# The second pass of a first stage rearranged, and TensorE's last jump made to wait, in a fused attention and gated feed-forward kernel

## The chip, the cores and the metric

The kernel runs on one core of one Trainium2 chip. The metric is the device time of one execution in microseconds (us). A core has five engines that run their own instruction streams and wait for one another through semaphores: TensorE (PE in the profile; PEld is its weight load), VectorE (DVE), ScalarE (ACT), GpSimd (POOL) and SyncE (SP). SP computes nothing here; it issues DMAs in a fixed order.

## The reference

One layer: normalise the rows of `x` (2048 rows of 640), run attention with 32 heads over given keys and values, run a gated feed-forward on the same normalised rows, and join the two.

```python
x = A_x                                   # [1, 2048, 640] bfloat16
xn = _layernorm(x, axis=-1)
# attention: H = 32 heads, Dh = 192, 2048 keys
q = (xn @ wq).reshape(B, Sq, H, Dh).transpose(0, 2, 1, 3)
scores = einsum("bhqd,bhkd->bhqk", q, k_cache) * (Dh ** -0.5)
s = (softmax(scores) @ v_cache) ... @ wo
# feed-forward: F = 1536
g = silu((silu(xn @ w1) * (xn @ w3)) @ w2)
return x + s * g
```

## The kernel before, in words

**Tiling.** The 2048 query rows are 16 row tiles of 128 (index `i`), or four blocks of 512 (`qb`). A head's 2048 keys are 16 key tiles, worked in 8 pairs (`p` from 0 to 7): tile `p` and tile `p + 8` together. One *group* is one head and one block of 512 queries, that is 8 pairs.

**One pair** is a call of `advance` (L525). It issues the scores on TensorE (`scores`, six matmuls, L467) into a PSUM tile `st2` of which there are two; the exponential on ScalarE (`weights`, L474, 1.1 us), which frees that PSUM tile; and it appends eight *pieces* (`values`, L499; two matmuls each, L507) of the product with the values to the list `parts`. Pieces are taken off the front of the list until a set number is left, so TensorE works on products of an earlier pair while ScalarE forms the exponential of this one. How many are left is the threshold in L542: 12, or 14 or 16 where other work goes in between.

**The end of a group.** The products of a group lie in two PSUM banks (`ob0`, `ob1`). When the last piece of a bank is issued, `evict` (L477) makes VectorE sum the bank's two halves into `osum` (L483, about 0.95 us); the next group's first pieces write the same bank and wait for it. The rest of it, a reciprocal (L489) and a multiplication that normalises (L490), goes to the list `late`. `drain_late`, at the start of `advance`, issues what is in `late` as soon as both banks are there.

**The start.** While the first groups run, the rows aren't all normalised yet. For a row tile `i` these steps follow each other: `ln_stats` (three instructions on VectorE, L223 and L224), `ln_root` (two on ScalarE for several tiles at once, L230 and L233), `ln_scale` (one on VectorE, L241, 128x640), `dma_turn` (a transposing DMA that SP issues, L252, into `xnT`). The first four tiles are turned on TensorE instead, between *fillers*: matmuls on constants that write a scratch bank (`keep_busy`, L210 to L217), 17 in all, issued before and between the first real matmuls. The projection of a head's queries for one block (`project_chunk`, L326; two parts of ten matmuls) needs the four turned tiles of that block. Behind it, ScalarE casts it out of PSUM, GpSimd copies rows (L359, L365), VectorE takes maxima (L353), and GpSimd sums over partitions (L424) to give a bound `nb` that the exponentials of that group read.

**The order by hand.** In this stage each instruction stands in its engine's program order as written (`pin`). The first eight groups are worked in the order

```python
order = ((0, 0), (1, 0), (0, 1), (0, 2), (0, 3), (1, 1), (1, 2), (1, 3))   # (head, qb); n is the place in it
```

and two tables say what is issued besides: `extras[(n, p)]` goes at the end of pair `p` of the `n`-th group's `advance`, `posts[(n, p)]` right after it. The *second pass* is `n = 1`: head 1, block 0. At its pair 5 the projection of head 0, block 1 begins, whose rows are tiles 4 to 7; its second part goes at pair 6 (list `seconds`). Between the two parts ScalarE holds a marker that waits for the end of the first.

**The end.** The output is formed row tile by row tile (`output_tile`, L804 for the matmuls, L809 and L811 on VectorE, L813 the store). The last tile is worked in two pieces, of 512 and 128 columns, each stored by itself from SP. Then all engines load a flag (`redo`) and jump over a part that is run only when the flag is set (L958); in this kernel's runs it isn't. A hint marks TensorE's jump as likely taken, and the engines meet at the end of the program (L1010).

Of the kernel before, what the change touches and what calls it, by code (L numbers as in the profile page):

```python
# [9 lines left out]
ALU = mybir.AluOpType  # L10
# [13 lines left out]
def _pieces(n, maxw=512):  # L24
    k = -(-n // maxw)
    w = -(-n // k)
    return [(c, min(c + w, n)) for c in range(0, n, w)]


def _kernel_impl(ctx, tc, A_x, A_k_cache, A_v_cache, A_wq, A_wo, B_w1, B_w3, B_w2, out):  # L30
    nc = tc.nc
    _, SQ, D = A_x.shape
    _, H, SK, dh = A_k_cache.shape
# [7 lines left out]
    NPAIR = NKT // 2  # L41
# [23 lines left out]
    pin = tc.keep_in_program_order  # L65
# [102 lines left out]
    with ExitStack() as actx:  # L168
# [12 lines left out]
        mv = lnx.tile([P, NQT, nc.vector.BN_AGGR_DIM], F32, name="mv")  # L181
        x_all = lnx.tile([P, NQT, D], BF16, name="x_all")
# [25 lines left out]
        one_l, one_r = (nc.const_aps.tensor(1.0, (P, w), BF16) for w in (P, 512))  # L208

        def keep_busy(n, out=None, behind=None):  # L210
            for _ in range(n):
                mm = pin(nc.tensor.matmul(fill[:, 0, :] if out is None else out, lhsT=one_l, rhs=one_r, start=True, stop=True))
                if behind:
                    tc.add_manual_dep(mm.ins, behind.ins.name,
                                      mybir.DependencyInfo(mybir.DependencyClass.Sync, mybir.DependencyReason.DATA),
                                      reason="not all at once")
                    behind = None  # L217
# [8 lines left out]
        rstd = {}  # L226
# [9 lines left out]

        scaled = {}

        def ln_scale(i):
            scaled[i] = xnp.tile([P, D], BF16, tag="xn", name="xn")  # L240
            pin(nc.vector.tensor_scalar(out=scaled[i][:], in0=x_all[:, i, :], scalar1=mv[:, i, 0:1], scalar2=rstd[i],  # L241
                                        op0=ALU.subtract, op1=ALU.mult))

        def ln_turn(i, pool, tag, cp):
# [6 lines left out]
        def dma_turn(i):  # L251
            pin(nc.sync.dma_start_transpose(out=xnT[:, i, :, :], in_=scaled.pop(i)[:]))  # L252

        def scale_and_turn(i):
            ln_scale(i)
            dma_turn(i)

        def stats_on_scalar(i):
# [266 lines left out]
        def advance(hd, qb, p, extra=None, st2=None, hold=False):  # L525
            def drain_late():
                while len(late) > 1:
                    late.pop(0)()
                    if len(late) == 1:
                        late.pop(0)()  # L530

            casts_first = p == 2 and (hd["h"] == H - 1 or (hd["h"], qb) == (1, NQB - 1)) and seconds
            if not casts_first:
                drain_late()
            first = (hd["h"], qb, p) == (0, 0, 0)
            pT2 = weights(scores(hd, qb, p) if st2 is None else st2, hd["nb"][qb], (0, 256, 512, 1024) if first else (0, 1024))
            parts.extend(values(hd, qb, p, pT2, first))
            while seconds:
                seconds.pop(0)()
            if casts_first:  # L540
                drain_late()
            while len(parts) > (16 if extra and p == 1 else 14 if extra or hold else 12):  # L542
                parts.pop(0)()
            if extra:
                extra()
# [66 lines left out]
        def complete_third():  # L612
# [19 lines left out]
            (0, 2): ((ln_root, 4), (scale_and_turn, 4), (scale_and_turn, 5), (key_maxima, 1, 0), (folded_maxima, 1)),  # L632
            (0, 4): ((join_maxima, 1), (next_bound, 1, 0)),
            (0, 5): ((ln_stats, 6), (ln_stats, 7)),
            (1, 0): ((ln_root, 6),),
            (1, 1): ((scale_and_turn, 6), (scale_and_turn, 7), (load_x, nc.sync, 12, 16)),
            (1, 2): ((ln_stats, 8), (ln_stats, 9)),
            (1, 3): ((ln_stats, 10), (ln_stats, 11)),
            (1, 4): ((ln_root, 8, 4), (scale_and_turn, 8), (scale_and_turn, 9)),
            (1, 5): ((scale_and_turn, 10), (scale_and_turn, 11)),  # L640
            (2, 2): ((ln_stats, 12), (ln_stats, 13)),
            (2, 3): ((ln_stats, 14),),
            (2, 4): ((ln_stats, 15),),
# [8 lines left out]
        def first_passes(n0, n1):  # L652
            for n in range(n0, n1):
                h, qb = order[n]
                for p in range(NPAIR):
                    todo = extras.get((n, p))
                    advance(heads[h], qb, p, (lambda: [f(*a) for f, *a in todo]) if todo else None,
                            early.pop(0) if early else None, (p == 0 and (n, 1) in extras) if n else p > 1)
                    for f, *a in posts.get((n, p), ()):
                        f(*a)  # L660
                    if n >= 6 and p > 2 and key_slots:
                        key_maxima(2, *key_slots.pop(0))
                    if p > 4 and gated:
                        gated.pop(0)()
                    if (n, p) == (7, 6):
                        assert not key_slots
                        finish_head(2)
                if n == 7:
                    while gated:
                        gated.pop(0)()  # L670
# [124 lines left out]
    def output_tile(pools, i, oT, xt):  # L795
        dsb, _, dps = pools
        split = i == NQT - 1
        to = nc.sync if split else nc.scalar
        ps_s = [dps.tile([P, 1024], F32, tag="st2", name="ps_s") for _ in range(2 if split else 1)]
        cuts = ((0, 512), (512, D)) if split else DP  # L800
        pieces = [(ps_s[-pi if split else 0][:, pi * 512:pi * 512 + c1 - c0], c0, c1) for pi, (c0, c1) in enumerate(cuts)]
        order = [(k, q) for q in pieces for k in range(OC)] if split else [(k, q) for k in range(OC) for q in pieces]
        for k, (ps, c0, c1) in order:
            pin(nc.tensor.matmul(ps, lhsT=oT[:, k, :], rhs=wo_sb[:, k, c0:c1], start=(k == 0), stop=(k == OC - 1)))  # L804
        res = dsb.tile([P, D], BF16, tag="res", name="res")
        for ps, c0, c1 in pieces:
            w = c1 - c0
            tmp = dsb.tile([P, 512], F32, tag="tmp", name="tmp")
            pin(nc.vector.scalar_tensor_tensor(out=tmp[:, 0:w], in0=ps, scalar=0.25, in1=g_all[:, i, c0:c1],  # L809
                                               op0=ALU.mult, op1=ALU.mult))  # L810
            pin(nc.vector.tensor_tensor(out=res[:, c0:c1], in0=tmp[:, 0:w], in1=xt[:, c0:c1], op=ALU.add))  # L811
            if i >= NQT - 7:
                stored = to.dma_start(out=out2[i * P:(i + 1) * P, c0:c1], in_=res[:, c0:c1])  # L813
                if split and c0 == 0:
                    tc.add_manual_dep(stored.ins, acc["out"].ins.name,
                                      mybir.DependencyInfo(mybir.DependencyClass.Sync, mybir.DependencyReason.DATA),
                                      reason="the tiles ahead are stored ahead")
                acc["out"] = stored
        if i < NQT - 7:
            to.dma_start(out=out2[i * P:(i + 1) * P, :], in_=res[:])  # L820
# [16 lines left out]
    with ExitStack() as dctx:  # L837
        dsb = dctx.enter_context(tc.tile_pool(name="dsb", bufs=3))
        otp = dctx.enter_context(tc.tile_pool(name="otp", bufs=3))
        pools = (dsb, otp, ps_st)  # L840
        with tc.issue_after(acc["store"].ins):
            tiles = [load_tile(pools, i) for i in range(3)]
        for qb in range(NQB):
            if qb + 1 < NQB:
                for fl in range(1 if qb == 0 else 0, FC - FCP):
                    ffn_hidden(qb + 1, fl, tail_ps("ps_gu"))()
            for i in range(qb * 4, qb * 4 + 4):
                ffn_out(i)
            if qb + 2 < NQB:
                load_hT(qb + 2)  # L850
            if qb == 0:
                worst = fsb.tile([P, 1], F32, tag="worst", name="worst")
                pin(nc.vector.tensor_reduce(out=worst[:], in_=rl_all[:], axis=AX.X, op=ALU.max))
                bad = fsb.tile([P, 1], BF16, tag="bad", name="bad")
                pin(nc.vector.tensor_scalar(out=bad[:], in0=worst[:], scalar1=RL_MAX, scalar2=None, op0=ALU.is_gt))
            if qb == 1:
                ps_b = ps_st.tile([P, 1024], F32, tag="st2", name="ps_b")
                pin(nc.tensor.matmul(ps_b[:, 0:1], lhsT=ones_bf[:], rhs=bad[:], start=True, stop=True))
                pin(nc.vector.tensor_copy(out=flag_i[:], in_=ps_b[:, 0:1]))
        for i in range(NQT - 1):  # L860
            output_tile(pools, i, *tiles.pop(0))
            if i + 3 < NQT:
                tiles.append(load_tile(pools, i + 3))
        with tc.block():
            tc.mark_branch_hint_location("redo", "LikelyTaken", (mybir.EngineType.PE,))
            output_tile(pools, NQT - 1, *tiles.pop(0))
    pstack.close()

    redo = nc.values_load(flag_i[0:1, 0:1], min_val=0, max_val=P)
# [145 lines left out]
```

## Time and profile before

| | us |
|---|---|
| median of three runs | 1941.05 |
| lowest and highest | 1939.77 and 1941.24 |
| the profiled execution, in all | 1939.65 |
| its span, first to last instruction | 1937.9 |
| granted TensorE clock | 0.999 |
| scores (L467), six groups by operands, each matmul | 0.376 |
| exponential (L474), 1016 of them | 1131.2 in all, 1.114 each |
| products (L507), 16384 of them | 861.4 in all, 0.243 each |
| scaling of a row tile on VectorE (L241) | 0.4 |
| GpSimd row copies, 64x512 and 64x1024 | 0.62 and 1.03 to 1.09 |

The span is the time from the first to the last instruction of the profiled execution; the rest of its 1939.65 us lies around it. In the tables a line gives the kernel's line, the engine, the operation, and `out<-in` by the program's names; `[0.71 <-DMA xnT<-xn]` says that the engine stood idle for 0.71 us before it, until the DMA that writes `xnT` had landed. Matmuls are pipelined, so one of 0.376 us starts every 0.1 to 0.2 us.

### The profile page before, as it was taken

The page shows a single profiled execution, that of the slowest core. Times are in us where ns is not written, and L with a number is a line of the kernel's source. Part 1 is how long each engine was busy: PE and PEld are TensorE (multiplying, and loading weights), DVE is VectorE, ACT ScalarE, POOL GpSimd, SP SyncE. Part 2 cuts the span into 40 slices and gives each one's busy share as a digit, 9 for nine tenths or more (in the row PEclk, how much of TensorE's full clock was granted, in tenths as well). Part 3 has the DMA queues.
Part 4 walks back from the last instruction along what each step waited for, and adds up shares of the span by engine and source line. Part 5 has one row for each costly group of instructions (what it writes and reads, how often), then busy time and mean ns, then how long its engine had stood idle before and what let it go on. Part 6 is the DMA issues. An engine that isn't in the chain of part 4 may idle for free.

```text
span 1937.9 us, 60322 instructions
## 1 busy us (share of the span) xinstructions
PE 1928.0 (99%) x27227; PEld 1359.5 (70%) x27228; DVE 1022.3 (53%) x1861; ACT 1278.7 (66%) x1296; POOL 414.3 (21%) x634
## 2 busy tenths in 40 slices
PE   8999999999999999999999999999999999999998
PEld 5779866666666777766666666677776666677776
DVE  8475556565656565556555565555565544521111
ACT  6777777777777777777777777777777777210000
POOL 2422222222222222222222222222222110000000
PEclk9999999999999999999999999999999999999999
DMA  8532323232222222333423232323232102927782
GB/s 180 105 76 53 79 47 85 47 74 45 67 45 71 52 67 60 63 82 77 109 57 75 55 77 55 76 47 85 47 85 44 40 5 75 287 65 135 151 155 54
DMA packets 361575, 152.83 MB, mean 79 GB/s; under 512 B 312448, under 2 KB 355136, under 8 KB 361312
## 3 DMA queue, kind: packets, MB, share of 16 engines
q1 hardware_dynamic: 346736, 120.11, 28.7%
q0 software_dynamic: 7872, 23.60, 4.8%
q10 hardware_dynamic: 6704, 5.21, 1.0%
q8 instruction: 214, 3.51, 0.7%
q14 instruction: 49, 0.40, 0.1%
HBM read 56.23 MB, written 31.98 MB: 46 GB/s over the span
## 4 chain that ended last, share of the span: by engine, by line
PE 98%; SPq 1%; DVE 1%; DMA 0%; ACT 0%; POOL 0%; issue 0%; POOLq 0%
PE obank L507 35%; PE st L467 34%; PE ps L326 14%; PE ps_s L804 11%; PE ps_f L828 3%; PE ps_gu L310 1%; SPq L124 0%; PE ps_gu L326 0%; DMA KB<-in_A_k_cache_dram 0%; DVE st L223 0%; DVE osum L483 0%; ACT pT L474 0%; SPq L185 0%; DVE mv L224 0%; DVE st L396 0%
## 5 line engine op out<-in xcount | busy, mean ns | idle before, releaser
L474 ACT ACTIVATE pT<-st,nb 128x1024 bf16<-128x1024 f32 x1016 | 1131.2, 1114 | 346.0 <-PE st L467 339.8
L507 PEld LDWEIGHTS <-pT 64*128 64x128 bf16 x16384 | 731.1, 94 | 225.0 <-issue 0.9
L507 PE MATMUL obank<-vt,pT 64*128 64x193 bf16 x16384 | 861.4, 243 | 0.3
L483 DVE TENSOR_REDUCE osum<-obank 128x386 f32<-128x772 f32 x256 | 234.4, 957 | 584.7 <-PE obank L507 584.6
L467 PE MATMUL st<-qA,KA 64*128 64x512 bf16 x2048 | 398.2, 376 | 1.1 <-ACT pT L474 1.0
L467 PE MATMUL st<-qF,KB 64*128 64x512 bf16 x1024 | 385.0, 376 | 0.0
L467 PE MATMUL st<-qS,KC 64*128 64x512 bf16 x1024 | 384.9, 376 | 0.1
L467 PE MATMUL st<-qS,KB 64*128 64x512 bf16 x1024 | 384.9, 376 | 0.0
L467 PE MATMUL st<-qD,KC 64*128 64x512 bf16 x960 | 361.0, 376 | 0.0
L326 PE MATMUL ps<-xnT,w 64*128 64x512 bf16 x2520 | 315.8, 376 | 0.7 <-DMA xnT<-xn 0.7
L359 POOL COPY qS<-qA 64x512 bf16<-64x512 bf16 x256 | 159.6, 623 | 636.2 <-ACT qA L369 627.7
L467 PEld LDWEIGHTS <-KC 64*128 64x128 bf16 x1984 | 186.2, 94 | 104.9
L326 PEld LDWEIGHTS <-w 64*128 64x128 bf16 x2520 | 132.4, 94 | 110.3 <-issue 1.1
L804 PE MATMUL ps_s<-wo_sb,oT 128*128 128x320 bf16 (+2 forms) x1535 | 208.8, 299 | 0.1
L467 PEld LDWEIGHTS <-KB 64*128 64x128 bf16 x2112 | 193.4, 94 | 13.6 <-issue 0.6
L804 PEld LDWEIGHTS <-oT 128*128 128x128 bf16 x1536 | 148.4, 98 | 60.4
L490 DVE TENSOR_TENSOR ostage<-osum,rl_all 128x384 bf16<-128x384 f32 x256 | 158.0, 617 | 8.8
L467 PEld LDWEIGHTS <-KA 64*128 64x128 bf16 x2048 | 116.7, 93 | 17.4 <-issue 2.7
L105 POOL DMA_DIRECT2D w<-in_A_wq_dram x60 | 53.1, 885 | 286.2 <-PE ps L326 286.0
L370 DVE CAST qF<-ps 128x512 bf16<-128x512 f32 x120 | 82.9, 691 | 51.6 <-ACT qA L369 51.6
L809 DVE SCALAR_TENSOR_TENSOR tmp<-ps_s,g_all 128x320 f32<-128x320 f32 (+2 forms) x32 | 15.6, 488 | 176.0 <-PE ps_s L804 176.0
L353 DVE TENSOR_REDUCE st<-qA 128x1 f32<-128x512 bf16 x128 | 86.5, 676 | 8.7 <-ACT qA L369 8.7
(95 smaller groups left out, 1035.4 us busy)
## 6 DMA issues: line engine op xcount, KB each, us to landing
o_scr<-ostage SPq DMA_DIRECT2D x64, 384.0 KB, 2.7
vt<-in_A_v_cache_dram SPq DMA_DIRECT2D x31, 768.0 KB, 6.3
wo_sb<-in_A_wo_dram POOLq DMA_DIRECT2D x1, 7680.0 KB, 32.2
w<-in_A_wq_dram POOLq DMA_DIRECT2D x30, 160.0 KB, 3.4
hT_scr<-hblk SPq DMA_DIRECT2D x16, 256.0 KB, 2.9
xt<-in_A_x_dram POOLq DMA_DIRECT2D x16, 160.0 KB, 8.8
w<-in_B_w_dram POOLq DMA_DIRECT2D x30, 80.0 KB, 2.6
w<-in_A_wq_dram POOLq DMA_DIRECT2D x30, 80.0 KB, 2.7
```

Of the source, the lines that this page charges most:

```text
L105: return lambda eng: keep(eng.dma_start(out=w[:, :, c0:c1], in_=src[:, s0:s0 + c1 - c0].rearrange("(c p) d -> p c d", p=P)))
L326: mm = pin(nc.tensor.matmul(out[:, t * 512:(t + 1) * 512], lhsT=ws[t][ROWS[r], c, :], rhs=rows_of(qb, c, ROWS[r]), start=(ph == 0 and c == 0),
L353: pin(nc.vector.tensor_reduce(out=hd["st"][r0:P, 2 + s, qb:qb + 1], in_=src[r0:P, qb * 512:(qb + 1) * 512], axis=AX.X, op=ALU.max, apply_a ...
L359: return [lambda t=t: keep(nc.gpsimd.tensor_copy(out=hd["qS"][ROWS[t], qs], in_=hd["qA"][ROWS[1 - t], qs])) for t in range(2)]
L370: pin(cast(out=hd["qF"][:, qs], in_=ps[:, 512:1024]))
L467: pin(nc.tensor.matmul(st2[:, t * 512:(t + 1) * 512], lhsT=keys, rhs=q[ROWS[t], qs], start=(s == 0), stop=(s == 2)))
L474: pin(nc.scalar.activation(out=pT2[:, c0:c1], in_=st2[:, c0:c1], func=ACT.Exp, scale=SCALE, bias=nb[:]))
L483: pin(nc.vector.tensor_reduce(out=osum[:], in_=ob[:].rearrange("p t (j c) -> p j c t", j=2)[:, :, 0:DH + 1, :], axis=AX.X, op=ALU.add))
L490: pin(nc.vector.tensor_tensor(out=ostage[:, b * 2:b * 2 + 2, hg * DH:(hg + 1) * DH], in0=osum[:, :, 0:DH], in1=rl.unsqueeze(2).to_broadcas ...
L507: pin(nc.tensor.matmul(acc["o"][b][:, r, j * 256:j * 256 + DH + 1], lhsT=pT2[ROWS[r], t * 512 + i * P:t * 512 + (i + 1) * P], rhs=vt[ROWS[ ...
L804: pin(nc.tensor.matmul(ps, lhsT=oT[:, k, :], rhs=wo_sb[:, k, c0:c1], start=(k == 0), stop=(k == OC - 1)))
L828: pin(nc.tensor.matmul(ps[:, pi * 512:pi * 512 + c1 - c0], lhsT=hT[:, fc, qsl], rhs=w2_sb[:, fc, c0:c1], start=(fc == 0), stop=(fc == FC - ...
```

## The change

Five edits.

- **Fillers in halves.** `keep_busy` issues each filler as two matmuls of 256 columns instead of one of 512.
- **Scaling.** `ln_scale` and `scale_and_turn` take an engine. Row tile 6 is scaled on GpSimd, right after the root of tiles 6 and 7 at the end of pair 0 of the second pass, instead of on VectorE at pair 1. The root of tiles 8 to 11 and the scaling and turning of tiles 8 and 9 go from the end of pair 4 to the end of pair 5, where tiles 10 and 11 already were.
- **Normalising put back.** In the second pass the first group's normalising (`late`) isn't issued at pair 2, but at pair 6, the seventh.
- **Pieces held.** In the second and third group 16 pieces instead of 12 are left in the list at pair 1. (The new condition gives the same as before in all other groups.)
- **The last jump.** Behind the last output tile TensorE gets an empty instruction that waits for VectorE's last sum; the flag's load and the jump stand behind it.

```diff
         def keep_busy(n, out=None, behind=None):
-            for _ in range(n):
-                mm = pin(nc.tensor.matmul(fill[:, 0, :] if out is None else out, lhsT=one_l, rhs=one_r, start=True, stop=True))
+            to = fill[:, 0, :] if out is None else out
+            for c0, c1 in _pieces(512, 256) * n:
+                mm = pin(nc.tensor.matmul(to[:, c0:c1], lhsT=one_l, rhs=one_r[:, c0:c1], start=True, stop=True))
...
-        def ln_scale(i):
+        def ln_scale(i, eng=nc.vector):
             scaled[i] = xnp.tile([P, D], BF16, tag="xn", name="xn")
-            pin(nc.vector.tensor_scalar(out=scaled[i][:], in0=x_all[:, i, :], scalar1=mv[:, i, 0:1], scalar2=rstd[i],
+            pin(eng.tensor_scalar(out=scaled[i][:], in0=x_all[:, i, :], scalar1=mv[:, i, 0:1], scalar2=rstd[i],
                                         op0=ALU.subtract, op1=ALU.mult))
...
-        def scale_and_turn(i):
-            ln_scale(i)
+        def scale_and_turn(i, eng=nc.vector):
+            ln_scale(i, eng)
             dma_turn(i)
...
             casts_first = p == 2 and (hd["h"] == H - 1 or (hd["h"], qb) == (1, NQB - 1)) and seconds
-            if not casts_first:
+            put_back = (hd["h"], qb) == (1, 0) and p < NPAIR - 2
+            if not casts_first and not put_back:
                 drain_late()
...
-            while len(parts) > (16 if extra and p == 1 else 14 if extra or hold else 12):
+            while len(parts) > (16 if p == 1 and (extra or hold) else 14 if extra or hold else 12):
...
-            (1, 0): ((ln_root, 6),),
-            (1, 1): ((scale_and_turn, 6), (scale_and_turn, 7), (load_x, nc.sync, 12, 16)),
+            (1, 0): ((ln_root, 6), (scale_and_turn, 6, nc.gpsimd)),
+            (1, 1): ((scale_and_turn, 7), (load_x, nc.sync, 12, 16)),
             (1, 2): ((ln_stats, 8), (ln_stats, 9)),
             (1, 3): ((ln_stats, 10), (ln_stats, 11)),
-            (1, 4): ((ln_root, 8, 4), (scale_and_turn, 8), (scale_and_turn, 9)),
-            (1, 5): ((scale_and_turn, 10), (scale_and_turn, 11)),
+            (1, 5): ((ln_root, 8, 4), (scale_and_turn, 8), (scale_and_turn, 9), (scale_and_turn, 10), (scale_and_turn, 11)),
...
-                            early.pop(0) if early else None, (p == 0 and (n, 1) in extras) if n else p > 1)
+                            early.pop(0) if early else None, (p == ((n, 1) not in extras)) if n else p > 1)
...
-            pin(nc.vector.tensor_tensor(out=res[:, c0:c1], in0=tmp[:, 0:w], in1=xt[:, c0:c1], op=ALU.add))
+            acc["sum"] = pin(nc.vector.tensor_tensor(out=res[:, c0:c1], in0=tmp[:, 0:w], in1=xt[:, c0:c1], op=ALU.add))
...
             output_tile(pools, NQT - 1, *tiles.pop(0))
+            wait = pin(nc.tensor.nop())
+            tc.add_manual_dep(wait.ins, acc["sum"].ins.name,
+                              mybir.DependencyInfo(mybir.DependencyClass.Sync, mybir.DependencyReason.DATA),
+                              reason="what follows the jump is fetched behind the last rows")
```

## The prediction

> **What bounds the kernel now.** I read the first page of the profile first, then the busy times by stage, then the order of time around the one stage that isn't full, then the end.
>
> ```profile
> span 1937.9 us, 60322 instructions
> PE 1928.0 (99%) x27227; PEld 1359.5 (70%) x27228; DVE 1022.3 (53%) x1861; ACT 1278.7 (66%) x1296; POOL 414.3 (21%) x634
> PE 98%; SPq 1%; DVE 1%; DMA 0%; ACT 0%; POOL 0%; issue 0%; POOLq 0%
> ```
>
> TensorE is busy 1928.0 of 1937.9 us and nearly alone on the chain that ends last, so an edit can win only out of the 9.9 us in which it stands still, whatever it does elsewhere. The busy times by stage (stretch and its length, then busy us of PE, its weight loads, DVE, ACT, POOL, with instruction counts) say where those are.
>
> ```profile
> 24.00:44.00 20.00, 18.01 (x276) 12.68 (x272) 15.37 (x40) 14.03 (x18) 2.55 (x5) 1.00 0.85 147
> 44.00:70.00 26.00, 26.00 (x391) 18.42 (x387) 14.31 (x38) 20.90 (x24) 7.45 (x13) 1.00 0.65 110
> 70.00:1600.00 1530.00, 1530.00 (x23616) 1087.96 (x23613) 885.17 (x1571) 1170.55 (x1149) 385.25 (x581) 1.00 0.28 63
> 1724.00:1938.00 214.00, 208.90 (x1538) 148.37 (x1536) 31.11 (x66) 0.88 (x2) 7.02 (x13) 0.99 0.62 119
> ```
>
> From 44 us to 1724 us nothing is missing. What the change can reach is the 2.0 us lost between 24 and 44 us (the second pass, head 1) and the 5.1 us at the end, 4.9 of them after the last matmul (1932.95). The timeline of the second pass:
>
> ```profile
> 30.61 1.23 SPq L252 DMA_TRANSPOSE xnT<-xn  x1
> 33.43 1.25 PE L326 MATMUL ps<-xnT,w 64*128 64x512 bf16 x10 [0.71 <-DMA xnT<-xn]
> 33.88 0.21 DVE L224 BATCH_NORM_AGGREGATE mv<-st 128x2 f32<-128x12 f32 x1
> 34.12 0.30 ACT L230 ACTIVATE lv<-mv,eps_t 128x4 f32<-128x4 f32 x1 [2.06 <-DVE mv L224]
> 34.56 1.10 ACT L474 ACTIVATE pT<-st,nb 128x1024 bf16<-128x1024 f32 x1
> 34.69 1.51 DVE L241 TENSOR_SCALAR xn<-x_all,mv,rstd 128x640 bf16<-128x640 bf16 x4 [0.60 <-ACT rstd L233]
> 35.71 0.39 PE L467 MATMUL st<-qA,KA 64*128 64x512 bf16 x2 [1.03 <-ACT pT L474]
> ```
>
> Two stalls. The projection (33.43) waits 0.71 for the turned rows of tile 7. Then the scores at 35.71 wait 1.03 for an exponential that ScalarE began late, at 34.56, because the root of tiles 8 to 11 (34.12) stands ahead of it in ScalarE's order and waits 2.06 us for VectorE's statistics. VectorE is late for this reason:
>
> ```profile
> 26.16 1.86 DVE L483 TENSOR_REDUCE osum<-obank 128x386 f32<-128x772 f32 x2
> 27.94 0.79 DVE L241 TENSOR_SCALAR xn<-x_all,mv,rstd 128x640 bf16<-128x640 bf16 x2
> 28.65 0.16 DVE L489 RECIPROCAL rl_all<-osum 128x2 f32<-128x2 f32 x1
> 28.84 0.56 DVE L490 TENSOR_TENSOR ostage<-osum,rl_all 128x384 bf16<-128x384 f32 x1
> ```
>
> **Part by part.** *Fillers.* 17 fillers (11+2+1+1+2) become 34 of half the width, the same columns. Each of the 17 added matmuls costs nothing if its weight load hides, at most one 128x128 load (98 ns, the row of L804) if it does not: 1.1 us on the first eleven, which end ahead of a 1.14 us idle, the others beside idles of 0.38 and 0.24 us. Only the single one between two turned tiles (7.82) has no cover: up to +0.1; a shorter last piece could win as much. I take 0.
>
> *Tile 6 on GpSimd, one step earlier.* VectorE scales tiles 6 and 7 at 27.94, 0.4 us each, and SP issues their turns behind: from 28.40 (2.1 us) and 30.61 (1.23 us); by their times to landing (4.1 and 2.7 us) they land at 32.5 and 33.3. Now GpSimd scales tile 6 as soon as ScalarE's root (26.66, 0.20 us) is there, at 26.9. No such row exists on POOL; its nearest are copies, 0.62 us for 512 columns and 1.03 to 1.09 for 1024, so 0.72 for 640 by the line between them, and twice that, 1.44, if the two arithmetic steps cost two passes. POOL has idle time until 38.37, so nothing queues behind it. SP's turn of tile 6 then starts 0.75 to 0.05 us earlier. VectorE still scales tile 7, at 28.0, well before SP wants it. But the two turns before it, issued at 23.11 and 25.08, landed only at 31.3 and 31.9 (8.2 and 6.8 us): the DMA engines were behind, and turned tiles then came 0.6 us apart. By that cadence tile 7 lands at 33.1 at best, not 32.55. So the gain is 0 to 0.71 us; I take 0.2, the cadence being the nearer row.
>
> *Root of tiles 8 to 11 one pair later, normalising put back.* The exponential of pair 5 no longer stands behind the root, so it starts at 32.1, right behind its scores (31.40 plus 0.65). The scores at 35.71 could then follow the projection's first part directly, where 1.2 us lie between by the starts (33.43 plus 1.08 is 34.51): gain 1.2. The four normalising steps (0.16+0.56, twice; 1.4 us) leave VectorE's order at 28.65, so its statistics of tiles 8 to 11 end by 33.3 (x_all lands only at 29.2, and four tiles of 1.0 us follow) instead of 34.1. They come back at pair 6, and there they are on a path: the root waits behind ScalarE's marker for the first part's end (34.3), then root 0.5, scaling 1.5, normalising 1.4, and only then the query maximum, at 37.8, where its input would be ready at 36.7. GpSimd's copies run beside it, and the second maximum is wanted at 38.05 and starts at 38.45, so 0.4 us of the 1.1 reach the bound and the exponential waiting for it (41.34 before, 40.1 after). The loss is bounded by 0 (if the copies hide it) and 1.1. SP's four turns of tiles 8 to 11 keep their order; they are wanted only at 46.7 and landed at 42.5.
>
> *Pieces held.* Eight matmuls move from pair 1 to pair 2 in the second and third groups. The 0.26 us stall in the products at 26.5 (1.12 us for 16 instead of 0.85) goes, but both sums end on VectorE at 28.0 whatever TensorE does, and the held pieces then reach the second bank at 27.83: 0.2 us of waiting takes its place. In the third group the wait for the exponential at 40.1 does the same. Gain 0 to 0.4, taken as 0.1.
>
> Start in sum: 0.2 + 1.2 + 0.1 - 0.2 (what the late bound gives back by the time the next group runs full) = 1.3 us, between 0 and 2.4.
>
> *TensorE's last jump.* The views of the end (throughput in 50 ns slices from 1934 to 1936; the line of the jump; the last two stores):
>
> ```profile
> GB/s 0 0 0 0 0 0 0 0 0 31 154 220 144 57 10 328 0 0 0 0 0 0 164 0 0 0 0 0 0 0 0 0 0 0 5 5 10 5 10 5
> q8 instruction: 1, 0.02, 3.0%
> L958 PEldq COMPARE_BRANCH  x1: 1603/1603/1603, 1932.4 to 1932.4; - x1
> DMA to landing us min/median/max: 2.0/2.6/3.2
> ```
>
> The last store's rows move at 1934.45 to 1934.75, then a 16 KB instruction packet (the 328) takes one DMA engine, and the last rows come 1.0 us late, at 1935.7 to 1936.0. This store lands 3.2 us after issue, the one ahead 2.0. The jump ends at 1934.0 and the packet follows 0.77 us later. A wait for the last sum (1933.32 plus 0.29) ends at 1933.65; behind it on TensorE stand the flag's load (0.49) and the jump, so the jump ends at 1934.3 at the earliest, and its packet starts at 1935.1, behind rows that are through at 1934.75. Then the store lands 1.2 us sooner, and since every engine's end follows it, the span loses 1.2. Bounds: 0 (the packet is still served first; it must have held the engine before the slice in which it shows) and 1.25; a later TensorE matters only past 1936.9, where SP collects it. I take 1.2, because the shift of 0.3 us equals the length of the rows' burst.
>
> [...]
>
> Sum: 1937.9 - 1.3 - 1.2 = 1935.4 us of span. The profiled execution took 1939.65 in all, 1.4 below the median of 1941.05 (the three runs spread over 1.5). Taken from the median: **1938.5 us**.
>
> **Rivals.** *The end keeps its wait:* the packet still goes ahead of the rows, as it did with a jump only 0.3 us earlier: 1941.05 - 1.3 = 1939.75. For it speaks that its data were seen only after the rows' burst, though it blocked them. *The start's gain turns into a new wait:* VectorE's normalising and the exponential's bound eat the 1.3; only the end wins: 1939.85. Against it: 0.6 us of slack beside GpSimd's copies. *All stalls of the second pass vanish:* the DMA engines are less behind with SP's earlier issue, 0.7 more from the projection, 0.9 from the waits at 39.8 and 41.8: 1936.9. *GpSimd is slow at its first arithmetic:* if the scaling takes T, tile 6 is turned from 26.9+T instead of 28.40, and everything behind follows. With 2.4 us won elsewhere (1.1+1.2+0.1) it costs more than it brings from T = 3.9. At 7.5 us the kernel takes 1941.05 + 3.6 = 1944.7. Against it: POOL's first 1024-column copy took 1.03 us, no more than the later ones.
>
> [...]
>
> **How the numbers follow.** Forecast 0.45, end keeps its wait 0.22, start gives nothing 0.13, all stalls vanish 0.11, slow GpSimd 0.05, neither part does anything (1941) 0.04. A measurement of this kernel tells about 0.2% (3.9 us) from no change: faster is below 1937.2, slower above 1944.9. Faster is most of "all vanish" and the low edge of the forecast, 0.16; slower is half of the slow GpSimd and a mishap not seen, 0.06; the rest 0.78. The range goes from the fourth case to the run spread above the second and third: 1936.8 to 1941.5; the forecast's own is 1937.3 to 1939.7.
>
> **What would show it.** In the profile after: no root ahead of the sixth exponential, and scores directly behind the projection's first part; a POOL row of the scaling under 1.5 us; a wait for xnT still there, 0.4 to 0.8 us; a last store that lands in 2.0 us, not 3.2. It is wrong if TensorE waits over 1 us for xnT, if the exponential of the third group starts after 41, or if the store stays at 3.2.

## The result and the profile after

The change made the kernel slower: 1951.92 us (median of six runs, 1951.2 to 1954.1) against 1939.91 us for the kernel before (six runs, 1939.09 to 1941.24), a ratio of 1.0063 with a 95% interval of 1.005 to 1.0076. Forecast were 1938.5 us, in a range that ended at 1941.5. The profiled execution of the changed kernel is the slowest of its six (1954.1 us); that of the kernel before took 1939.65. So the two spans below lie 14.3 us apart, and the medians 12.0.

The first page and the stages of the changed kernel (a stretch and its length, then busy us of PE, its weight loads, DVE, ACT and POOL, the granted TensorE clock, the DMA share and GB/s):

```profile
span 1952.2 us, 60363 instructions
PE 1934.3 (99%) x27244; PEld 1364.8 (70%) x27245; DVE 1021.8 (52%) x1860; ACT 1277.8 (65%) x1296; POOL 416.3 (21%) x635
24.00:44.00 20.00, 13.51 (x176) 8.56 (x174) 9.90 (x29) 9.56 (x13) 3.08 (x3) 0.84 0.58 127
44.00:70.00 26.00, 20.34 (x266) 14.33 (x264) 13.41 (x35) 13.26 (x17) 4.52 (x8) 0.86 0.18 42
70.00:1600.00 1530.00, 1530.00 (x23606) 1088.99 (x23604) 884.09 (x1571) 1170.47 (x1150) 387.71 (x585) 1.00 0.29 65
```

From 70 to 1600 us TensorE is full in both kernels. The loss lies between 24 and 70 us, but for 0.7 us of a later start, and in both stages two things are new: TensorE stands still for over 5 us, and its granted clock is below 1. What TensorE waited for between 30 and 60 us (us in total, times, longest), and when GpSimd worked (start, duration):

```profile
PE ps L327 <- DMA xnT<-xn: 6.3, 1, 6.3
PE st L468 <- ACT pT L475: 5.6, 1, 5.6
```

```profile
25.23 0.38 POOL L425 PARTITION_ALL_REDUCE nb<-ns  x1 [0.77 <-DVE ns L423]
33.19 2.52 POOL L242 TENSOR_SCALAR xn<-x_all,mv,rstd 128x640 bf16<-128x640 bf16 x1 [7.58 <-PE st L468]
45.70 0.61 POOL L360 COPY qS<-qA 64x512 bf16<-64x512 bf16 x1 [9.99 <-ACT qA L370]
46.36 0.60 POOL L366 COPY qD<-qF 64x512 bf16<-64x512 bf16 x1
46.91 0.61 POOL L360 COPY qS<-qA 64x512 bf16<-64x512 bf16 x1
53.80 0.40 POOL L425 PARTITION_ALL_REDUCE nb<-ns  x1 [6.28 <-DVE st L224]
```

The scaling of tile 6 has its last input when ScalarE writes the root at 27.62, but it begins at 33.19; the sum over partitions has its input at 48.06 (the row of L423, 47.91 plus 0.15), but it begins at 53.80. The releasers that the rows name, TensorE's scores and VectorE's statistics, have nothing to do with these instructions: the inference from semaphores found the last event it knew. What does stand there are instructions that count as no work, two to configure GpSimd ahead of the scaling and two ahead of the sum:

```profile
L242 POOLq MODIFY_POOL_CONFIG  x2: 79/81/83, 25.5 to 25.5; - x2
```

```profile
L425 POOLq MODIFY_POOL_CONFIG  x2: 4/4/4, 47.7 to 47.8; - x2
```

In the kernel before and in the changed one, the line that loads a library for the sums over partitions (`load_library`, L72) shows as such a pair, at 0.8 us:

```profile
L72 POOLq MODIFY_POOL_CONFIG  x2: 11/11/11, 0.8 to 0.9; - x2
```

So I read the two pairs as GpSimd swapping the routines that it has ready, and call a pair with the idle time behind it a swap: there, to the scaling (7.6 us from the pair at 25.5), and back, to the sum (6.0 us from the pair at 47.8). The rows show the configuring instructions and the idle time behind them, not what happens in it; the experiments test when this time is paid. TensorE's two waits (6.3 and 5.6 us) are each about as long as a swap, and behind the first of them TensorE runs at half clock for 4.6 us, behind the second for 5.9 us (in a row, the clock stands after the five engines, ahead of the DMA share):

```profile
33.20:39.70 6.50, 0.22 (x6) 0.00 (x0) 1.20 (x5) 0.93 (x1) 2.51 (x1) 0.83 0.29 54
39.70:44.40 4.70, 4.65 (x24) 1.97 (x26) 1.60 (x6) 1.52 (x3) 0.00 (x0) 0.51 0.47 139
49.60:55.40 5.80, 0.21 (x4) 0.00 (x0) 5.61 (x16) 1.16 (x2) 0.40 (x1) 0.92 0.22 68
55.40:61.30 5.90, 5.89 (x54) 4.39 (x55) 0.73 (x3) 3.19 (x3) 0.00 (x0) 0.50 0.01 3
```

The sum of it: 0.7 us of a later start (first scores at 14.16 for 13.49), 5.6 us more wait for xnT (6.3 for 0.7), 5.6 for the late bound, and about half of 4.6 and of 5.9 us to the low clock, 5.3 together; that is 17.2. Off it go 1.0 for the scores' wait that is gone and 1.35 at the end (last matmul to the end of the span: 3.58 us after, 4.93 before). Left are 14.9, for 14.3 us between the spans. Marks on TensorE's way close it better: the first scores start 0.7 us later than before, the projection's first part 6.3 (39.75 for 33.43), the products behind its second part 7.3 (44.77 for 37.44), those of the next group 15.7 (65.20 for 49.48), and the last matmul ends 15.7 later as well (1948.67 for 1932.95). Less 1.35 at the end this is 14.4.

### The profile page after: what moved, and what is told of

Same layout as the page of the kernel before. It is cut to its first block, busy times and chain, and to the rows that moved or that the text cites. A ratio compares the mean times of both kernels' runs of the same rounds, so it can differ in the third digit from the quotient of the medians.

```text
span 1952.2 us, 60363 instructions
## 1 busy us (share of the span) xinstructions
PE 1934.3 (99%) x27244; PEld 1364.8 (70%) x27245; DVE 1021.8 (52%) x1860; ACT 1277.8 (65%) x1296; POOL 416.3 (21%) x635
## 4 chain that ended last, share of the span: by engine, by line
PE 98%; DVE 1%; SPq 0%; DMA 0%; POOL 0%; issue 0%; ACT 0%; POOLq 0%
PE obank L508 34%; PE st L468 34%; PE ps L327 14%; PE ps_s L805 11%; PE ps_f L829 3%; PE ps_gu L311 1%; PE ps_gu L327 0%; SPq L124 0%; DVE st L224 0%; DVE osum L484 0%; DMA w<-in_A_wq_dram 0%; DMA xnT<-xn 0%; POOL xn L242 0%; PE pa L311 0%; DVE st L354 0%
## 5 line engine op out<-in xcount | busy, mean ns | idle before, releaser
L468 PEld LDWEIGHTS <-KB 64*128 64x128 bf16 x2112 | 193.7, 94 | 14.5 <-issue 1.6
L491 DVE TENSOR_TENSOR ostage<-osum,rl_all 128x384 bf16<-128x384 f32 x256 | 157.2, 614 | 8.8
```

The lines of the kernel that those rows point to most:

```text
L468: pin(nc.tensor.matmul(st2[:, t * 512:(t + 1) * 512], lhsT=keys, rhs=q[ROWS[t], qs], start=(s == 0), stop=(s == 2)))
L491: pin(nc.vector.tensor_tensor(out=ostage[:, b * 2:b * 2 + 2, hg * DH:(hg + 1) * DH], in0=osum[:, :, 0:DH], in1=rl.unsqueeze(2).to_broadcas ...
```

## The experiments

All twelve kernels are edits of the changed kernel or of the one before, and each was timed beside the kernel before. Two theories stood against each other at first: GpSimd's swap, or the new order of the second pass.

**Tile 6 on VectorE (e1_vector).** From the changed kernel:

```diff
-            (1, 0): ((ln_root, 6), (scale_and_turn, 6, nc.gpsimd)),
+            (1, 0): ((ln_root, 6), (scale_and_turn, 6)),
```

> The changed kernel with tile 6 scaled on VectorE, at the same place. Theory (a swap of GpSimd's routines: the first scaling and then the first sum over partitions behind it each begin some 5.6 us after their inputs are there): the wait for xnT falls from 6.3 us to under 1, the wait of the next group's exponential for its bound from 6.7 to about 1, and the span from 1952.2 to about 1935.5, that is 2 to 3 us under the kernel before (ratio 0.9985). Rival (the new order: normalising put back, root one pair later, held pieces): the waits stay, the kernel stays over 1945.

Measured: 1937.38 us beside 1940.03, ratio 0.9987 (0.9978 to 0.9996), span 1935.8. Both waits are gone; what TensorE still waited for between 14 and 60 us:

```profile
PE obank L508 <- DMA vt<-in_A_v_cache_dram: 0.7, 1, 0.7
PE st L468 <- POOL qS L360: 0.6, 1, 0.6
PE obank L508 <- DVE osum L484: 0.3, 1, 0.3
```

The engine that scales one row tile makes a difference of 14.5 us of 1952, and all the other edits together gain 2.65 us (0.8 to 4.3 by the interval).

**GpSimd's scaling alone (e2_gpsimd_alone).** From the kernel before, tile 6 scaled by `nc.gpsimd` at its old place, pair 1.

> The kernel before with one edit: tile 6 scaled on GpSimd at its old place. Theory (swap of routines): 10 to 15 us slower than before, with two waits of 5 to 7 us on TensorE at about 33 and 46 us. Rival (the new order does it): within 2 us of before, since the scaling itself takes 2.5 us instead of 0.4.

Measured: 1953.48 us, ratio 1.0069 (1.0054 to 1.0085), with TensorE's waits of 5.7 us for xnT and 5.3 us for the exponential. The loss needs none of the other edits.

**Two tiles on GpSimd (e4_two_on_gpsimd).** From the changed kernel, tile 7 scaled on GpSimd too.

> The changed kernel with tile 7 scaled on GpSimd too, right behind tile 6. Theory (a swap, paid once for each change of routine): the second scaling begins as the first ends, 2.5 us long; the kernel is 2 to 3 us slower than the changed one, about 1954.5. Rival (every arithmetic instruction of this kind starts 5.6 us late on GpSimd): the second begins 5.6 us after the first, the kernel is about 8 us slower than the changed one, about 1960.

Measured: 1953.94 us in one run. The row holds both scalings:

```profile
33.30 5.01 POOL L242 TENSOR_SCALAR xn<-x_all,mv,rstd 128x640 bf16<-128x640 bf16 x2 [7.77 <-DVE st L224]
```

One idle time of 7.77 us, then 5.01 us for two: the swap is paid at the change, not by each instruction. TensorE's wait for xnT grew by 1.4 us only (7.7 for 6.3), since SP turns tile 6 while tile 7 is scaled. The time of this one run can't be told from the changed kernel's six (1951.2 to 1954.1), so the 2 to 3 us that the theory added aren't shown.

**The way back, earlier (e5_back_early).** From the changed kernel, with a sum over one spare column behind the scaling:

```diff
-            (1, 0): ((ln_root, 6), (scale_and_turn, 6, nc.gpsimd)),
+            (1, 0): ((ln_root, 6), (scale_and_turn, 6, nc.gpsimd), (spare_sum,)),
...
+        def spare_sum():
...
+            pin(nc.gpsimd.memset(a[:], 0.0))
+            pin(nc.gpsimd.partition_all_reduce(b[:], a[:], P, bass_isa.ReduceOp.add))
```

> The changed kernel with a sum over partitions of a spare column on GpSimd right behind the scaling of tile 6, its result unused. Theory (the swap back is paid by the first sum): it is paid at 36 to 41 us, where GpSimd has nothing else to do, and the later sum begins within 1 us of its input; the second wait of TensorE (5.8 us at 49.6) and the half clock behind it go, the first (6.6 us at 33.2) stays: span about 1945. Rival (GpSimd is slow in anything once it has run this arithmetic, or the bound is late for another reason): the second wait stays, about 1952.

Measured: 1945.42 us in one run, span 1943.6.

```profile
42.03 0.40 POOL L607 PARTITION_ALL_REDUCE spare_b<-spare_a  x1 [6.11 <-issue]
45.15 0.61 POOL L360 COPY qS<-qA 64x512 bf16<-64x512 bf16 x1 [2.71 <-ACT qA L370]
45.82 0.82 POOL L366 COPY qD<-qF 64x512 bf16<-64x512 bf16 x1
46.59 0.61 POOL L360 COPY qS<-qA 64x512 bf16<-64x512 bf16 x1
48.05 0.38 POOL L425 PARTITION_ALL_REDUCE nb<-ns  x1 [0.85 <-DVE ns L423]
```

The spare sum pays the way back (6.11) while GpSimd has nothing else to do, and the bound comes 0.85 us behind its work instead of 6.28. The profiled span is 8.6 us shorter, by one execution of each kernel. 8.1 of it lie where the second wait was: from the products behind the projection (44.77 there, 44.22 here) to those of the next group (65.20 and 56.54). So the way back cost its wait of 5.6 us and the half clock behind it.

**The way there, earlier (e6_there_early).** From the changed kernel, with a scaling of one spare column right behind the first sum over partitions (25.4).

> The changed kernel with a scaling of one spare column on GpSimd right behind the first sum over partitions, ahead of tile 6's scaling, its result unused. Theory A (the swap begins when the first instruction of the other kind is free to start): it begins at 25.6 instead of 27.6, tile 6's scaling at about 31.3 instead of 33.2, the first wait is 1.9 us shorter, span about 1950.3. Theory B (it begins with the configuring instruction at 25.5 and takes 7.6 us): the scaling still begins at 33.2, span 1952.

Measured: 1954.82 us in one run.

```profile
33.82 0.40 POOL L611 TENSOR_SCALAR spare_c<-mv,rstd 128x1 f32<-128x1 f32 x1 [8.00 <-PE st L468]
34.22 2.53 POOL L242 TENSOR_SCALAR xn<-x_all,mv,rstd 128x640 bf16<-128x640 bf16 x1
```

Theory A fell: the spare instruction had its inputs long before, and yet nothing began before 33.8. The swap's time counts from the configuring instruction (25.7), which already stood right behind the sum; the changed kernel's wait for the root at 27.6 ran beside it and cost nothing. Theory B had 7.6 us from that instruction; it was 8.1 here, and the scaling of tile 6 began at 34.2 instead of 33.2.

**The swap in calm (e11_swap_in_calm).** From the kernel before, with both spare instructions in head 5, where nothing waits for GpSimd and the DMA engines are at a share of 0.01 to 0.04:

```diff
+                    if (h, qb, p) == (5, 1, 4):
+                        pin(nc.gpsimd.tensor_scalar(out=spares[0][:], in0=place[:, 0:1], scalar1=place[:, 0:1],
+                                                    scalar2=eps_t[:], op0=ALU.subtract, op1=ALU.mult))
+                    if (h, qb, p) == (5, 2, 4):
+                        pin(nc.gpsimd.partition_all_reduce(spares[1][:], eps_t[:], P, bass_isa.ReduceOp.add))
```

> The kernel before, with a scaling of one spare column on GpSimd in head 5, block 1, pair 4, and a sum over partitions of a spare column one block later, results unused: a swap there and back where nothing waits for GpSimd and the DMA engines are calm. [...] Theory B (the way there is longer in itself): 7.1 to 8.0 us again. [...]

Measured: 1939.85 us beside 1940.38, ratio 0.9998 (0.9989 to 1.0008).

```profile
303.75 0.40 POOL L747 TENSOR_SCALAR spare<-place,eps_t 128x1 f32<-128x1 f32 x1 [7.14 <-issue]
307.41 1.27 POOL L360 COPY qS<-qA 64x512 bf16<-64x512 bf16 x2 [3.27 <-ACT qA L370]
308.74 0.61 POOL L366 COPY qD<-qF 64x512 bf16<-64x512 bf16 x1
315.22 0.40 POOL L750 PARTITION_ALL_REDUCE spare<-eps_t  x1 [5.87 <-issue]
```

The way there takes 7.1 us in calm too, as theory B had it; under the loads at 25 us (DMA share 0.76 from 25.5 to 33.2 us in the changed kernel) it took 7.2 to 8.1, and whether those loads add anything isn't shown. In every run the way there is the first of its kind in the execution, so whether a second one would be as long isn't shown either. The copies between the two ran as usual, at 0.61 to 0.64 us, so here they waited for no swap. Where nothing waits, both swaps cost no time that these runs can tell from none.

**The other parts.** *TensorE's last jump alone (e3_jump_alone)*, from the kernel before:

> The kernel before with one edit: TensorE's last jump waits for the last sum. Theory (the instruction packet goes behind the last rows): the last store lands 1.5 us after its issue instead of 3.2 and the kernel is 1.2 to 1.5 us faster (ratio 0.9993). [...]

Measured: 1939.44 us beside 1940.03, ratio 0.9996 (0.9987 to 1.0005). In its profile the last store landed after 1.46 us, and last matmul to end took 3.58 us instead of 4.93; all ten profiles with the waiting jump show 3.58 to 3.60. By time no gain is shown: the interval includes no change. A reason can be read from the profiles without the waiting jump, which don't all pay: in four of them (before, e2_gpsimd_alone, e11_swap_in_calm, e12_root_alone) the store took 3.16, 3.41, 1.47 and 1.5 us. So the theory holds for the profiles in which the packet meets the rows. Whether that changes with the kernel or from one execution of the same kernel to the next isn't shown, and the size of the average gain stays open between 0 and 1.35.

*The late root alone (e12_root_alone)*, from the kernel before:

```diff
-            (1, 4): ((ln_root, 8, 4), (scale_and_turn, 8), (scale_and_turn, 9)),
-            (1, 5): ((scale_and_turn, 10), (scale_and_turn, 11)),
+            (1, 5): ((ln_root, 8, 4), (scale_and_turn, 8), (scale_and_turn, 9), (scale_and_turn, 10), (scale_and_turn, 11)),
```

> The kernel before with one edit: the root and the scaling of tiles 8 to 11 at pair 5. Theory (the root's place alone carries the start's gain): the 1.0 to 1.2 us between the projection's first part and the scores goes, the median is 1.2 to 1.6 us under before (ratio 0.9993), and 0.4 to 1.4 us above the kernel that has the waiting jump too. Rival (most of the 3.3 us that the two edits brought is the jump's): under 0.6 us faster.

Measured: 1938.91 us beside 1940.25, ratio 0.9992 (0.9983 to 1.0001). The 1.34 us are what the theory had, but the interval just includes no change. The profile shows the mechanism: the scores follow the projection's first part directly (34.57 behind 33.50) and no longer wait for the exponential. Here the last store took 1.5 us without the waiting jump.

*Both together (e8_root_and_jump):*

> The kernel before with two edits: the root and the scaling of tiles 8 to 11 at pair 5, and TensorE's last jump waiting for the last sum. Theory (these two carry the gain): the scores' wait of 1.0 us at 34.3 goes, the wait for xnT of 0.7 us stays, the last store lands in 1.5 us; 2.0 to 2.6 us faster than before (ratio 0.9988). Rival (the gain needs tile 6 scaled sooner, the held pieces and the halved fillers): 1.3 us or less faster.

Measured: 1937.08 us beside 1940.42, ratio 0.9984 (0.9975 to 0.9993). This beats both kernels. The two edits alone gained 0.59 and 1.34 us, together 3.34; each of these gains is uncertain by about 1.7 us, so that they add to more than their sum isn't shown. The second pass there:

```profile
33.18 1.25 PE L326 MATMUL ps<-xnT,w 64*128 64x512 bf16 x10
34.26 0.40 PE L467 MATMUL st<-qA,KA 64*128 64x512 bf16 x2
34.56 0.30 ACT L230 ACTIVATE lv<-mv,eps_t 128x4 f32<-128x4 f32 x1 [0.73 <-DVE mv L224]
35.12 1.12 ACT L474 ACTIVATE pT<-st,nb 128x1024 bf16<-128x1024 f32 x1
```

The scores (34.26) follow the projection's first part (33.18) directly, with the root behind them. The wait for xnT is under 0.1 us here; in the profile before it was 0.7, in other profiles with the same old place of tile 6 it was 0 to 0.5, so this one moves from profile to profile. That it would stay, as the theory had it, was a miss.

*Normalising at its old place (e7_not_put_back)*, the changed kernel with tile 6 on VectorE and without `put_back`:

> The changed kernel with tile 6 scaled on VectorE and the normalising at its old place, pair 2. Theory (put back, the normalising stands ahead of the query maximum on VectorE and runs beside GpSimd's row copies): GpSimd's first two copies take 0.6 us again instead of 0.87 and 0.83, the scores' wait at 38.5 falls from 0.7 to about 0.2 to 0.4 us, the bound comes 0.4 to 0.5 us sooner, and the kernel is 0.3 to 0.6 us faster than with the normalising put back. Rival (put back, it lets the statistics end sooner, and that counts): slower by 0.5 to 1.4 us, with a wait for the root or for xnT.

Measured: 1937.26 us, ratio 0.9985 (0.9976 to 0.9995); by time it can't be told from e1_vector. By the profiles it can. GpSimd's copies in e1_vector, with the normalising put back, beside VectorE's (36.92 and 37.59):

```profile
37.08 0.87 POOL L360 COPY qS<-qA 64x512 bf16<-64x512 bf16 x1 [11.87 <-ACT qA L370]
38.01 0.83 POOL L366 COPY qD<-qF 64x512 bf16<-64x512 bf16 x1
38.79 0.61 POOL L360 COPY qS<-qA 64x512 bf16<-64x512 bf16 x1
```

and in e7_not_put_back, without:

```profile
36.93 0.61 POOL L360 COPY qS<-qA 64x512 bf16<-64x512 bf16 x1 [11.73 <-ACT qA L370]
37.59 0.61 POOL L366 COPY qD<-qF 64x512 bf16<-64x512 bf16 x1
38.15 0.61 POOL L360 COPY qS<-qA 64x512 bf16<-64x512 bf16 x1
```

Put back, the normalising lengthens two copies and the scores wait 0.5 us more for them. The gain set against it isn't there: in e1_vector the statistics end at 34.1, not at the 33.3 of the forecast, and where the normalising stands at its old place (e8_root_and_jump) the later root waits 0.73 us for them, but no wait of TensorE comes of it.

*Held pieces (e9_and_hold)*, added to e8_root_and_jump:

> The kernel with the late root and the waiting jump (e8_root_and_jump), and the held pieces added. Theory (VectorE's two sums end when they end, the waits only move): the stalls in the products at 27.2 (0.26 us) and 40.8 (0.23) turn into others of like size, 0 to 0.3 us in sum. Rival (the hold covers the sums): both stalls go, 0.4 to 0.5 us sooner at 45 us than without.

Measured: 1937.81 us, ratio 0.9989 (0.9979 to 0.9998). Of the two stalls of 0.26 and 0.23 us in the products, 0.24 and 0.18 are left (by the starts of neighbouring matmuls): the waits only move.

*Fillers in halves (e10_and_fillers)*, added to e8_root_and_jump:

> The kernel with the late root and the waiting jump, and the fillers halved. Theory (the fillers end in idle time): the first real matmuls of the projections (L310 before, at 9.4 us) start as far behind VectorE's last copy as before, nothing changes beyond the spread of the start. Rival (34 weight loads, or a different start of the clock): the start of the scores moves by 0.3 us or more.

Measured: 1938.02 us in one run. The first projection starts 0.15 us behind VectorE's last copy, as in the kernel before (9.43 and 9.28). The scores start at 14.27, which is later than before by the 0.3 us of the rival and more (13.49). But the fillers are not needed for that: without them halved the scores started at 13.49 to 14.12 in seven profiles, with them halved at 13.47 to 14.27 in seven, and here TensorE stood still for 0.72 us for a load of weights by DMA. Nothing else was found.

## Why the prediction was wrong

**What bounds the kernel, and where the change can act: right.** Between 70 us and the end nothing was gained or lost except in the last microseconds.

**"Tile 6 on GpSimd, one step earlier": here it failed.** The step priced the scaling from the nearest POOL rows, which are copies (0.72 to 1.44 us). It measured 2.52 us, 0.40 for one column, so about 3.3 ns for each column against 0.8 to 0.9 in the copies. By the prediction's own reckoning (a loss only from 3.9 us on) that alone would not have made the kernel slower; no run shows it by itself. What the step left out is the wait ahead of the scaling: 5.6 us from the time its inputs are there. So a term taken as a gain of 0.2 us turned into a loss of 14.5 (e1_vector). The copies were the wrong neighbours, since they ran without such a wait between the two swaps (0.61 to 0.64 us each, e11_swap_in_calm). The right sign stood in the code: it loads a library for the sums over partitions (`load_library`, L72), and no row of the profile before has GpSimd doing arithmetic on a tile.

**"POOL has idle time until 38.37, so nothing queues behind it": wrong as well.** Behind it queue the copies, and the sum that makes the bound; the swap back lies exactly between them. This second payment, 8.1 us by e5_back_early, stood in no rival.

**The rival "GpSimd is slow at its first arithmetic": right place, a third of the price, a chance of 0.05.** From its inputs to its end the scaling took 8.1 us (27.62 to 35.71), near the 7.5 of this rival, a value that no row of the profile before shows; but the rival made 3.6 us of loss out of it, for 12.0 between the medians: it had neither the second payment nor the half clock. It was argued away with the first 1024-column copy, which took no longer than later ones. Measured from the configuring instruction, the swaps took 5.6 to 6.1 us back and 7.1 to 8.1 us there.

**Half clock behind a wait: not thought of.** In the five profiles with a swap before 60 us, TensorE's waits of 5.3 to 7.7 us were each followed by 2.8 to 5.9 us of work at a clock of 0.50, which cost about half of that, 1.4 to 3.0 us. The clock fell 2.4 to 5.2 us into a wait (4.0 and 4.7 us in the changed kernel). What sets these times isn't shown. In the kernel before, where TensorE's longest wait was 1.14 us, the clock stands at 1.00 up to the last matmul.

**The root one pair later: right.** Forecast 1.2 us, and e12_root_alone measured 1.34 in the medians (the interval goes from a loss of 0.2 to a gain of 3.3); the wait that it was to remove is gone in its profile. **Normalising put back:** the loss through the query maximum was forecast at 0.4 us and is 0.5 by the scores' wait, though by the lengthened copies and not by the maximum alone; the gain set against it isn't there. **Pieces held:** forecast 0.1, found 0.1 in the stalls. **Fillers:** forecast 0, found 0, by one run. **The last jump:** forecast 1.2, and 1.35 in the profiles, but only beside those that met the packet. Without the GpSimd step the forecast's sum would have stood: 1938.5 forecast from 1941.05, or 2.55 us, and e1_vector gained 2.65. That the two are so close is in part luck: the interval of e1_vector's gain is 0.8 to 4.3 us, and single terms (the normalising, the jump's average) weren't what was forecast.

## What to carry to other kernels

Before an instruction is moved to GpSimd, look in the code for a library that is loaded for the engine's other instructions, and in a profile for `MODIFY_POOL_CONFIG` ahead of it and of them; a swap between a scaling and a sum over partitions took 5.6 to 8.1 us each way here, and the wait shows up behind an instruction that seems to have its inputs, under the name of an engine that has nothing to do with it. If the move must be, put a spare instruction of each kind where nothing waits for GpSimd (e5_back_early did so for the way back; no run here hid the way there from the scaling that needs it). And price a wait on TensorE as long as those here (5.3 to 7.7 us) with the half clock behind it: it made 5.6 us into about 8.

## What wasn't expected of the hardware

The swap starts with the configuring instruction, not with the first instruction behind it that is free to start, so other waits run beside it (e6_there_early: 8.1 us from the pair at 25.7, with the inputs there long before). The two directions differ: in calm 7.1 us there and 5.6 back, each measured from its pair of configuring instructions. Where VectorE's normalising ran beside them, two of GpSimd's copies took 0.87 and 0.83 us instead of 0.61 (e1_vector and e7_not_put_back), and one of the normalising's own multiplications (L491) took 0.77 us instead of 0.56: the instructions of both engines got longer, by 0.2 to 0.3 us. And whether an instruction packet meets the last store changes from one profile to the next: 1.35 us at the end of the span between two profiles, beside 3.4 us between the fastest and the slowest run of the kernel before (1938.13 to 1941.57 in one comparison).
